# Polysketch attention and a multiplicative FFN on one core: queries, later keys and outputs transposed in 32x32 blocks by VectorE, from loads by head

## The chip, the cores and the metric

The kernel runs on one core of a Trainium2 chip. The metric is the device time of one execution in microseconds (us), lower is better. The engines are TensorE (PE; PEld are its weight loads), VectorE (DVE), ScalarE (ACT), GpSimd (POOL) and SyncE (SP), which issues the transfers. A profile is of one of the timed executions, and its span is 1.7 to 1.9 us shorter than that execution's time.

## The reference

```python
# q, k, v: (B=4, H=4, S=1088, D=32); S1, S2: (8, 32)
def phi(x):
    a = np.einsum('rd,bhsd->bhsr', S1, x)
    b = np.einsum('rd,bhsd->bhsr', S2, x)
    return np.einsum('bhsi,bhsj->bhsij', a, b).reshape(*x.shape[:-1], r * r)
q_p, k_p = (phi(q), phi(k))
kv = np.einsum('bhsf,bhsd->bhfd', k_p, v)
z = np.sum(k_p, axis=2)
num = np.einsum('bhsf,bhfd->bhsd', q_p, kv)
den = np.einsum('bhsf,bhf->bhs', q_p, z)[..., None] + 1e-06
x = (num / den).transpose(0, 2, 1, 3).reshape(B * S, H * D)      # 4352 tokens x 128
# w1, w2: (128, 1024); w3: (1024, 1024); w_out: (1024, 128), float64
out = ((x @ w1) * (x @ w2) @ w3) @ w_out
```

Nothing nonlinear stands between w3 and w_out, so the kernel multiplies the two once into one matrix w3o and saves the largest product. The weights come as float64 words; ScalarE and VectorE turn them into float32 in the kernel (raw, cv_c, cv_m, w3c in the profile).

## The kernel before

The tokens are worked off in nine groups: two halves of 512 tokens for each of four batches, and a last group of 256 with the 64 left-over tokens of each. A query goes through a long chain: transpose, projection, denominators, features, and the product with the keys' sums, which gives xT, the FFN's input. The FFN of a group is 8 pairs of products a and b, a VectorE product ab of each pair, and 8 products ps_o that add up the output, transposed. These are the transposes, each a copy, four products with the identity and a second copy:

```python
    def natural(t, half):                      # keys and queries: gather 512 tokens on ScalarE
        n = work.tile([128, 4, H, D], F32, tag="nat", name="nat")
        nc.scalar.copy(n, bview(t[:, 0, 4 * half], [[D, 4], [NJ * D, H], [1, D]]))
        return n.rearrange("p j h d -> p j (h d)")
    # ... in k_feat
        def tr():
            chunks = state.pop("chunks")
            ps = psum.tile([128, 512], F32, name="ps_kt", **banks)
            for j in range(nj):
                nc.tensor.transpose(ps[:, j * 128:(j + 1) * 128], chunks[j], ident)
            kT = work.tile([128, 512], F32, tag="kT", name="kT")
            nc.scalar.copy(kT[:, :nj * 128], ps[:, :nj * 128])
    # ... in q_steps
        def tr():
            ps = psum.tile([128, 512], F32, tag="t", name="ps_qt")
            for j, c in enumerate(s["src"]):
                nc.tensor.transpose(ps[:, j * 128:(j + 1) * 128], c, ident)
            s["qT"] = wtile("qT", bufs=2)
            nc.scalar.copy(s["qT"], ps[:, :n])
    # ... the FFN's output
    def ffn_o(g, c):
        _, n, _ = groups[g]
        if c == 0:
            o_ps[g] = psum.tile([DM, 512], F32, tag="out", name="ps_o")
        nc.tensor.matmul(o_ps[g][:, :n], w3o[:, c], ab_sb.pop((g, c))[:, :n], start=c == 0, stop=c == NC - 1)
        if c == NC - 1:
            o_ps[g, "sb"] = work.tile([DM, 512], F32, tag="ob", bufs=1, name="ob")
            nc.scalar.copy(o_ps[g, "sb"][:, :n], o_ps[g][:, :n])

    def ffn_out(g):
        _, n, dst = groups[g]
        ps = psum.tile([128, 4, DM], F32, tag="h", bufs=3, name="ps_ot")
        nj = n // 128
        for j in range(nj):
            nc.tensor.transpose(ps[:, j], o_ps[g, "sb"][:, j * 128:(j + 1) * 128], ident)
        oT = work.tile([128, 4, DM], F32, tag="oT", name="oT")
        nc.scalar.copy(oT[:, :nj], ps[:, :nj])
        dst(oT)
```

A first part, up to group 0's last pair, has a fixed order on every engine; after it a scheduler chooses the order on each engine. In the first part `gs` are the Gram products of batch 0's keys, `kv` the products of key features and values (both ps_kvz in the profile), `pause(n)` n dummy products that keep TensorE's clock up, and `f[c]` the product pairs of group 0:

```python
    run_all([sk_words, sketch_pairs, nat0, peak, sketch_T, tr0, nat1, tr1, pause(4), ab0, ab1, r_nat, r_tr, first, second,
             sketch_P_mm, r_ab, pause(3), gs0, kp0, gs1, kp1, q_nat, kv0, r_kp, kv1, kvr, q_tr, pause(5),
             # ... (fin1 .. phi of the first queries)
             w_out[0][1], n_dens2, f[4], n_phi, w_out[1][1], f[5], n_phT, f[6], n_nd, f[7]])
    run(merge(ffn_steps(1, 16), k_steps(1), w_out[2:]))     # from here on the scheduler orders
```

`w_out` is the list of steps that convert w_out (wo) and w3, multiply them and copy w3o.

## Time and profile before

| | before |
|---|---|
| time, median of 3 runs | 321.59 us (320.5 to 321.72) |
| span of the profile | 317.9 us |
| start: to where group 0's last product ab begins | 56.5 us |
| second stage: to where the last copy of w3o begins | 54.5 us |
| third stage: to where the last output's copy out of PSUM begins | 200.4 us |
| tail: to the end | 6.5 us |

The four stages are cut by the same events in every kernel here, so that their lengths can be set side by side. The first line of the page gives busy time, share of the span and number of instructions of each engine.

```profile
PE 296.4 (93%) x2143; PEld 176.8 (56%) x2143; DVE 188.0 (59%) x482; ACT 141.6 (45%) x277; POOL 7.1 (2%) x12
```

Two lines of the list of TensorE's waits (us in total, times, longest):

```profile
PE ps_ph L735 <- DVE ph L726: 1.6, 2, 1.2
PE ps_c L673 <- POOL q L649: 1.5, 2, 0.8
```

The second are two waits of 0.76 us in the third stage, from 167.5 and 226.9 us on, for a step of GpSimd in the query chain: nearly all of its idle time. The first lie in the start, 0.34 us at 31 us and 1.24 us at 49 us. The chain of waits in the start (start, us, engine, tile):

```profile
12.66 1.98 PE ps_kvz L508 x99
14.65 1.36 issue
16.01 1.67 PE ps_kvz L508 x61
```

The key products begin at 12.66 and end at 17.68 us, with 1.36 us in the middle in which TensorE waits for nothing that the profile shows.

### The profile page before, as it was taken

Reading aid. Unit: us, or ns where it says so; the run is one execution under the profiler, and the core shown is the slowest. Engines: PE = TensorE matmul, PEld = TensorE weight load, DVE = VectorE, ACT = ScalarE, POOL = GpSimd, SP = SyncE. Lnnn points to the kernel's source line nnn. Section 1 sums busy time; section 2 is a strip of 40 time slices with the busy share of each in tenths; the row PEclk is TensorE's granted clock in tenths of the full one; section 3 lists DMA queues with packets and bytes.
Section 4 is the critical chain, followed back from the end, with each engine's and each line's share of the span. In section 5 each row is a group of like instructions: output and inputs, shape, how many; then the busy total and the mean of one; then the engine's idle time right before and its main releaser. Section 6 shows DMA issues by size and latency. Waiting matters only on the chain.

```text
span 317.9 us, 5394 instructions
## 1 busy us (share of the span) xinstructions
PE 296.4 (93%) x2143; PEld 176.8 (56%) x2143; DVE 188.0 (59%) x482; ACT 141.6 (45%) x277; POOL 7.1 (2%) x12
## 2 busy tenths in 40 slices
PE   6898898589999999999999999999999999999992
PEld 4777433268777855655645456554545544444581
DVE  6769785899999463686537438443661662462120
ACT  4266674777976233632252471333324424423131
POOL 0000000000000000100001010000100100000000
PEclk9999999969999999999999999999999999999998
DMA  5539893166542000000000000000000000000000
GB/s 163 186 78 328 235 324 129 48 201 215 201 134 68 2 1 33 2 1 2 35 0 0 0 36 2 0 2 34 0 2 0 33 0 0 36 0 0 33 35 17
DMA packets 15065, 20.80 MB, mean 65 GB/s; under 512 B 4032, under 2 KB 11456, under 8 KB 15040
## 3 DMA queue, kind: packets, MB, share of 16 engines
q1 hardware_dynamic: 15040, 20.46, 20.3%
q8 instruction: 17, 0.28, 0.3%
q14 instruction: 8, 0.07, 0.1%
HBM read 18.22 MB, written 2.23 MB: 64 GB/s over the span
## 4 chain that ended last, share of the span: by engine, by line
PE 82%; DVE 9%; ACT 4%; issue 2%; POOL 1%; POOLq 0%; DVEq 0%; ACTq 0%
PE ps_o L810 19%; PE a_ps L797 18%; PE b_ps L801 15%; PE ps_kvz L508 5%; PE ps_w3o L403 5%; PE ps_wt L396 3%; PE ps_x L752 3%; PE ps_c L675 2%; PE ps_ab L452 2%; PE ps_c L673 2%; PE ps_ph L735 2%; PE idle_ps L190 2%; PE ps_ot L820 1%; ACT q L644 1%; ACT q L645 1%
## 5 line engine op out<-in xcount | busy, mean ns | idle before, releaser
L803 DVE TENSOR_TENSOR ab<-ffa,b_ps 128x512 f32<-128x512 f32 (+1 forms) x72 | 47.3, 657 | 68.2 <-PE b_ps L801 57.3
L799 ACT COPY ffa<-a_ps 128x512 f32<-128x512 f32 (+1 forms) x72 | 40.4, 560 | 75.9 <-PE a_ps L797 75.6
L797 PE MATMUL a_ps<-xT,w 128*128 128x512 f32 (+1 forms) x144 | 72.4, 585 | 1.0 <-ACT xT L755 0.7
L801 PE MATMUL b_ps<-xT,w 128*128 128x512 f32 (+1 forms) x144 | 70.1, 568 | 0.0
L810 PE MATMUL ps_o<-ab,w3o 128*128 128x512 f32 (+1 forms) x144 | 69.9, 582 | 0.0
L801 PEld LDWEIGHTS b_ps<-xT,w 128*128 128x128 f32 x144 | 27.1, 191 | 29.0 <-issue 25.0
L810 PEld LDWEIGHTS ps_o<-ab,w3o 128*128 128x128 f32 x144 | 24.9, 190 | 21.0 <-issue 19.8
L797 PEld LDWEIGHTS a_ps<-xT,w 128*128 128x128 f32 x144 | 24.4, 193 | 17.9 <-issue 11.1
L276 DVE TENSOR_REDUCE g_q<-qT 128x1 f32<-128x512 f32 (+1 forms) x9 | 5.9, 654 | 27.4 <-ACT qT L633 27.4
L403 PEld LDWEIGHTS ps_w3o<-wo,w3T 128*128 128x128 f32 x128 | 15.7, 192 | 3.4 <-issue 2.6
L737 ACT COPY pT<-ps_ph 128x512 f32<-128x512 f32 (+1 forms) x18 | 9.2, 565 | 18.5 <-PE ps_ph L735 18.5
L244 ACT ACTIVATE cv_c<-raw 128x512 f32<-128x512 f32 x22 | 15.0, 682 | 3.1 <-DVE w3c L257 2.6
L403 PE MATMUL ps_w3o<-wo,w3T 128*128 128x128 f32 x128 | 16.0, 275 | 0.0
L245 ACT ACTIVATE cv_m<-raw 128x512 int32<-128x512 uint32 x22 | 15.0, 681 | 0.9 <-DVE wo L260 0.4
L673 PE MATMUL ps_c<-Rf,q 128*128 128x64 f32 (+1 forms) x72 | 12.4, 263 | 2.6 <-POOL q L649 1.5
L190 PE MATMUL idle_ps<-zeros 128*128 128x256 bf16 x95 | 13.1, 295 | 1.7 <-DVE zeros L185 1.7
L675 PE MATMUL ps_c<-Rl,qT 128*128 128x96 f32 (+1 forms) x72 | 13.9, 284 | 0.0
L673 PEld LDWEIGHTS ps_c<-Rf,q 128*128 128x128 f32 (+1 forms) x72 | 10.4, 185 | 5.5 <-POOL q L649 2.4
L649 POOL TENSOR_TENSOR q<-qT,q 128x512 f32<-128x512 f32 (+1 forms) x6 | 6.4, 1074 | 267.4 <-ACT q L645 245.2
L508 PE MATMUL ps_kvz<-kk 128*32 128x64 f32 x256 | 8.6, 236 | 4.0 <-DVE kk L492 4.0
L462 DVE TENSOR_TENSOR kp<-ps_ab,b_sb 128x1024 f32<-128x1024 f32 x8 | 9.7, 1221 | 3.9 <-ACT b_sb L456 3.9
L190 PEld LDWEIGHTS <-zeros 128*128 128x128 bf16 x95 | 10.0, 108 | 3.4 <-DVE zeros L185 1.7
(162 smaller groups left out, 381.9 us busy)
## 6 DMA issues: line engine op xcount, KB each, us to landing
raw<-in_moe_w_dram SPq DMA_DIRECT2D x20, 512.0 KB, 4.8
k_sb<-in_k_dram SPq DMA_DIRECT2D x4, 512.0 KB, 4.0
v_sb<-in_v_dram SPq DMA_DIRECT2D x4, 512.0 KB, 4.1
q_sb<-in_q_dram SPq DMA_DIRECT2D x4, 512.0 KB, 5.8
out_dram<-oT SPq DMA_DIRECT2D x8, 256.0 KB, 2.0
raw<-in_moe_w_out_dram SPq DMA_DIRECT2D x2, 512.0 KB, 8.4
k_sb<-in_k_dram SPq DMA_DIRECT2D x4, 32.0 KB, 3.7
vr<-in_v_dram SPq DMA_DIRECT2D x4, 32.0 KB, 6.6
```

Source lines behind the costliest of these rows:

```text
L190: nc.tensor.matmul(idle_ps[:, :n], zeros[:, :128], zeros[:, :n], start=True, stop=True)
L244: nc.scalar.mul(x["c"], hi.bitcast(F32), 2.0 ** -112)
L245: nc.scalar.mul(x["m"].bitcast(I32), lo.bitcast(U32), 2.0 ** -29)
L403: nc.tensor.matmul(ps, w3T[ko][:, c], wo[:, c], start=(c == 0), stop=(c == NC - 1))
L508: nc.tensor.matmul(out[h * D:(h + 1) * D], lhs, rhs, start=start, stop=stop, skip_group_check=True)
L673: nc.tensor.matmul(C[rows, :2, j], s["q2"][:, cols], cols_of(Rf, b), start=True, stop=False, skip_group_check=True)
L675: nc.tensor.matmul(C[rows, :, j], s["qT"][:, cols], cols_of(Rl, b), start=False, stop=True, skip_group_check=True)
L797: nc.tensor.matmul(a_ps[:, :n], w1[:, cols], xT[key], start=True, stop=True)
L799: nc.scalar.copy(a_sb[:, :n], a_ps[:, :n])
L801: nc.tensor.matmul(b_ps[:, :n], w2[:, cols], xT[key], start=True, stop=True)
L803: nc.vector.tensor_mul(ab[:, :n], a_sb[:, :n], b_ps[:, :n])
L810: nc.tensor.matmul(o_ps[g][:, :n], w3o[:, c], ab_sb.pop((g, c))[:, :n], start=c == 0, stop=c == NC - 1)
```

## The change

VectorE transposes only inside 32x32 blocks (the prediction below cites the page that says so). A head has 32 columns, so if a load puts head h on the partitions 32h to 32h+31, and consecutive tokens beside each other in each partition, then one VectorE instruction over 128x512 gives what four products with the identity and two copies gave: (head, column) on the partitions, tokens in the free dimension. The tokens of a group come out in another order, which doesn't matter as long as the output's store puts them back. The outputs, which lie transposed in PSUM, go the same way: VectorE transposes straight out of PSUM, and four stores of 128 B runs put them in place. Only the last group's output stays with TensorE, stored by one transfer instead of four. Batch 0's keys stay with TensorE too. Later keys are loaded a second time for it, by head.

Two further parts: the start is reordered, so that the Gram products follow directly behind the key features (`first`, `second`), with the sketch's product later and two pauses gone; and five conversion steps move from behind the first part into it, so that all of wo and the words of w3's first piece are converted there. (With the two that stood there before they are the seven steps of `out_st`.)

```diff
+    def load_by_head(which, b):
+        n = {"q": NT, "k": 32}[which] * D
+        t = io.tile([128, n], F32, tag=which + "h", bufs={"q": 2, "k": 1}[which], name=which + "h")
+        if which == "q":
+            nc.sync.dma_start(t, bass.AP(tensor=q.tensor, offset=b * H * S * D, ap=[[n, 128], [1, n]]))
+        else:
+            for h in range(H):
+                nc.sync.dma_start(t[h * 32:(h + 1) * 32],
+                                  bass.AP(tensor=k.tensor, offset=(b * H + h) * S * D, ap=[[n, 32], [1, n]]))
+        by_head[which, b] = t
... (k_feat)
         def tr():
+            kT = state["kT"] = work.tile([128, 512], F32, tag="kT", name="kT")
+            if blocks:
+                nc.vector.transpose(bview(kT, [[1, 4], [128, nj], [4, 32]]), blocks())
+                return
... (queries)
+        def transpose(qT):
+            t = by_head["q", b]
+            nc.vector.transpose(qT, t[:, half * 512:(half + 1) * 512])
+            if half == 1:
+                nc.vector.transpose(qT_rest[:, b * SR:(b + 1) * SR], t[:, SM:])
+                if b + 2 < B:
+                    load_by_head("q", b + 2)
... (outputs)
-            nc.sync.dma_start(bass.AP(tensor=out.tensor, offset=(b * S + half * 4) * DM,
-                                      ap=[[NJ * DM, 128], [1, 4 * DM]]),
-                              oT.rearrange("p j d -> p (j d)"))
+            for i in range(4):
+                nc.sync.dma_start(bass.AP(tensor=out.tensor, offset=(b * S + half * 16) * DM + i * 32,
+                                          ap=[[NT * DM, 32], [DM, 16], [1, 32]]),
+                                  oT[i * 32:(i + 1) * 32].rearrange("p (T d) -> p T d", d=32))
...
-        if c == NC - 1:
-            o_ps[g, "sb"] = work.tile([DM, 512], F32, tag="ob", bufs=1, name="ob")
-            nc.scalar.copy(o_ps[g, "sb"][:, :n], o_ps[g][:, :n])
+        if c == NC - 1 and g < NG - 1:
+            oT = work.tile([128, 512], F32, tag="oT", name="oT")
+            nc.vector.transpose(oT, o_ps[g])
+            dst(oT)
+    def last_out():                            # the last group: TensorE, one store
+        ob = work.tile([DM, 256], F32, tag="ob", bufs=1, name="ob")
+        nc.scalar.copy(bview(ob, [[1, 4], [128, 2], [4, 32]]), o_ps[g][:, :n])
...
+    out_st, w_out = fs(w_out[:7]), w_out[7:]
-    run_all([sk_words, sketch_pairs, nat0, peak, sketch_T, tr0, nat1, tr1, pause(4), ab0, ab1, r_nat, r_tr, first, second,
-             sketch_P_mm, r_ab, pause(3), gs0, kp0, gs1, kp1, q_nat, kv0, r_kp, kv1, kvr, q_tr, pause(5),
+    run_all([sk_words, sketch_pairs, nat0, nat1, peak, sketch_T, tr0, tr1, ab0, ab1, r_nat, r_tr, first, second,
+             gs0, r_ab, kp0, gs1, kp1, gr, r_kp, sketch_P_mm, kv0, kv1, kvr, q_tr, pause(5),
...
-             pause(16), N_pair, ay1, q_rem, v0, n_nat, v1, ay2, n_tr, pause(30), split, dens, dens2, phi, j0, a0, j1, a1, phT, nd,
+             pause(16), N_pair, ay1, q_rem, v0, v1, ay2, n_tr, pause(30), split, dens, dens2, phi, j0, a0, j1, a1, phT, nd,
...
-             w_out[0][1], n_dens2, f[4], n_phi, w_out[1][1], f[5], n_phT, f[6], n_nd, f[7]])
+             out_st[0], n_dens2, f[4], out_st[1], n_phi, f[5], *out_st[2:4], f[6], n_phT, n_nd, *out_st[4:7], f[7]])
```

(The lines of `run_all` are broken at other places here than in the file; `last_out` is cut. Left out are small parts: the Gram products of the left-over keys become a step of their own, `gr`, and the copies that gather batch 0's keys share the buffers of w3's pieces.)

## The prediction

> **What bounds the kernel now.** I first read the busy digits and the granted clock by slice of the page (40 slices of 7.95 us), to see which engine is full in which stage.
>
> ```profile
> PE   6898898589999999999999999999999999999992
> ...
> DVE  6769785899999463686537438443661662462120
> ...
> PEclk9999999969999999999999999999999999999998
> ```
>
> The reader is to see four stages. Slices 0 to 6 (to about 57 us) are a start in which no engine is full: a chain of latencies. In slices 7 to 12 (57 to 101 us) VectorE stands at 8 and 9, and in slice 8 TensorE falls to 5 and its clock to 6. From slice 13 on TensorE is at 9 everywhere and VectorE at 3 to 8. The last slice is a tail. The page's chain that ended last agrees: PE 82%, DVE 9%, ACT 4%.
>
> For the second stage I asked for the busy time by stretch (per stretch: length, then busy us of PE, weight load, DVE, ACT, POOL, the clock, the DMA share, GB/s) and the list of waits (total us, times, longest).
>
> ```profile
> 60.00:70.00 10.00, 5.81 (x78) 4.15 (x78) 10.00 (x20) 6.49 (x12) 0.00 (x0) 0.66 0.56 166
> 70.00:80.00 10.00, 10.00 (x97) 8.04 (x96) 9.03 (x16) 8.15 (x16) 0.00 (x0) 1.00 0.66 211
> 80.00:101.00 21.00, 21.00 (x242) 15.72 (x242) 20.36 (x46) 16.83 (x33) 0.00 (x0) 1.00 0.45 148
> ```
>
> ```profile
> PE ps_kvz L508 <- DVE kk L492: 4.0, 1, 4.0
> ```
>
> VectorE is busy for all of 60 to 70 us, and TensorE idles 4.0 us of it in one piece, because the Gram products of batch 1 wait for kk, which stands in VectorE's queue behind the conversion of the output weights (wo). After that gap the clock is down: four transposes take 1.11 us in the chain at 66 us, against 0.44 later.
>
> For the long third stage I read the chain in order of time (start, us) and the groups by form (busy us, mean ns of one, idle before).
>
> ```profile
> 184.40 0.44 PE ps_ot L820 x4
> 184.83 0.44 PE ps_qt L631 x4
> ...
> 187.85 0.44 PE ps_kt L443 x4
> ```
>
> ```profile
> L820 PE MATMUL ps_ot<-ident,ob 128*128 128x128 f32 x34 | 5.2, 274 | 0.5 <-ACT ob L813 0.5
> L443 PE MATMUL ps_kt<-ident,nat 128*128 128x128 f32 x32 | 4.9, 277 | 1.2 <-ACT nat L108 1.2
> L631 PE MATMUL ps_qt<-ident,nat 128*128 128x128 f32 x32 | 4.9, 274 | 0.0
> ```
>
> The mean of 274 ns is the latency of one; they are pipelined, so what a set of four costs the engine is the chain's 0.44 us. They lie on the chain itself with nothing idle before them: whatever leaves TensorE here leaves the span.
>
> **What the Trainium skill says.** "VectorE: DVE Perf Modes", section "The three transpose paths": VectorE transposes only 32x32 blocks, 311 ns for 128x128 bf16 against TensorE's 390. No transpose of VectorE is in this trace. "Vector Engine (DVE) Microarchitecture Reference", section 3.8, has it sustain one element per cycle per lane. I therefore take the 0.69 us that this trace shows for other 128x512 f32 work on VectorE (L803: 686 ns), as an estimate. "TensorE: Matmul & The Clock Gate", Part 1: the clock halves after an idle window of about 3.4 us. The trace agrees: idle 4.0 us, granted 0.66 in that stretch, and 1.00 in every full one. "DMA: Bandwidth & Descriptors", Specifications: under 512 B a write is done as read-modify-write and misses line rate. The trace is only suggestive: 32 KB loads in 128 B runs took 3.7 to 6.6 us to land, 32 KB stores in 512 B runs 1.9 us, but the loads had other traffic beside them.
>
> **The change part by part.**
>
> (1) TensorE loses its transposes of queries (8 sets of four and 2 for the rest), of the keys of batches 1 to 3 (6 sets) and of outputs 0 to 7 (8 sets): 90 instructions at 0.11 us. In the third stage lie 6 of the query sets and the two, 4 key sets and 8 output sets: 18 x 0.44 + 0.22 = 8.1 us, all on the path. The other four sets lie in stages that TensorE doesn't bound.
>
> (2) ScalarE loses 14 natural-order copies (0.62), 8 qT copies (0.59) and the small one, 6 kT (0.58) and 8 each of ob and oT (0.585): 8.7 + 5.1 + 3.5 + 9.4 = 26.7 of its 141.6 us. By itself that is worth nothing in the third stage (ACT about 35% there). It shortens the head of each query chain: three times TensorE stood about 0.8 us before ps_c, waiting for q on POOL behind ACT's copies. I allow 0.5 us in all.
>
> (3) VectorE gains 22 transposes of 128x512 at 0.69 us and 4 small ones of 64 columns (about 0.22): 16.1 us, 188 to 204 us. In the third stage it has some 40% free. But its queue is in order: the transpose of an output waits there for the last ps_o product, and what stands behind it, the denominators of the queries, comes later. The bank of ps_o is single; the next group's first product must wait for the transpose where formerly it waited for an ACT copy of 0.59 us. Most times a pair of products (1.72 us) lies between. I set a loss of 1.5 us for such new waits.
>
> (4) Second stage: seven steps of the weight conversion, with both joins and adds of wo, move into the first part. At the pace of the chain (0.34 + 0.60 + 0.60) that takes 2 x 1.54 = 3.1 us of VectorE ahead of kk, and puts them into slots at 51 to 56 us where VectorE idled 2.16 and 2.23 us before two ab products. The two key transposes add 2 x 0.6. So kk should come some 3 us earlier, the gap of 4.0 us should become about 1, and the clock should stay up (it cost about 2 us: two sets of transposes at 1.11 for 0.44, and a product pair at 1.52 for 0.86). Against this, VectorE over 57 to 101 us is itself 96% full and wins only 3.1 - 1.2 = 1.9 us, unless it drops work done there early for batches 2 and 3. Between 1.9 and 5 us I choose 3.5.
>
> (5) Start: the Gram products follow the key features directly. Today kk is done at about 10.9 us and the Gram products begin at 12.6, behind pauses and the sketch product; keys' products end at 17.7. Taking away four pause products and letting the second natural copy run behind the first brings the ab products about 0.7 us forward. I expect the end of the key products at about 15.9 rather than 17.7 us (1.4 us of issue gap at 14.65 may stay). Against it, the second half's transpose and the rest of the queries now stand on VectorE in the chain at 25 us: 0.6 + 0.2 us. Net 1.0. At 49 us TensorE stood 1.24 us waiting for ph; the new order gives it product pair 6 first: another 1.0.
>
> (6) Tail: the last store is one transfer instead of four.
>
> ```profile
> 312.72 2.46 SPq L785 DMA_DIRECT2D out_dram<-oT  x4
> ```
>
> Each issue costs about 0.6 us, so the last left 1.8 us after the first: 1.8 us saved. The price is in the other outputs: four transfers a group, 2048 runs of 128 B instead of 128 of 2 KB. The queue was nearly empty after 101 us, and the last of these leaves some 8 us before the end.
>
> (7) Keys of batches 1 to 3 are loaded twice and queries in 4,352 B runs: 1.5 MB more, one third of it in the busy stretch of 24 to 48 us, where at some 300 GB/s it delays what follows by about 1.7 us. The list of waits shows no conversion waiting for its weights, so this is hidden.
>
> Sum: 8.1 + 0.5 - 1.5 + 3.5 + 1.0 + 1.0 + 1.8 = 14.4 us. 321.6 - 14.4 = 307.2; I say **307 us**.
>
> **The rivals.** (a) VectorE becomes a bound: if it needs two cycles an element for f32 transposes or for the strided key output, it gains some 28 us instead of 16, and the second stage gives back what it won; TensorE would then wait in the third stage at the four stretches where VectorE is at 6 to 8. The time would be about 313. For it: VectorE's 9s in slices 8 to 12. Against: the one element per cycle quoted above, and the 3s and 4s of most later slices. (b) A new wait takes the removed work's place: head-of-line waiting behind the output transposes delays the query chain and TensorE goes idle before ps_ph or ps_o; about 311. For it: today's chain lets a query chain pass at 104 to 124 us with barely any slack (VectorE's ph ends at 122.1 and TensorE takes it at 122.3). Against: the order after the first part is chosen again by the scheduler. (c) The small stores hold up the end: if 2048 runs took over 8 us, the last store would wait behind them; about 310. (d) The second stage gains fully, with the clock: 304 or less.
>
> **Range and chances.** Certain are the 8.1 us of part 1 and nearly so the 1.8 of the tail: 311.7 without anything else. The soft terms are the second stage (1.9 to 5), the start (0 to 3.5) and the new waits (0 to 5). All bad gives about 313, all good 301; I take 302 to 312.5. Two per cent is 315.2, which needs a slow VectorE transpose: faster 0.93, within 2% 0.06, slower 0.01.
>
> **What would show it.** Right, if the changed profile has TensorE's instructions 90 fewer and its digits still at 9 after slice 13, with that stage 7 to 9 us shorter; VectorE transposes of 128x512 near 0.69 us; the wait of ps_kvz for kk at 1 to 2 us and the clock digit of slice 8 back at 9; key products ending near 16 us; one last store. Wrong, if those transposes last 1 us or more, if TensorE shows new idle time before ps_o, ps_ph or ps_ab with VectorE as releaser, if the second stage is no shorter, or if the end waits for group 7's stores.

## More of the kernel before

The busy times by stretch, for exactly the third stage (length, then busy us and number for PE, PEld, DVE, ACT and POOL, the clock, DMA share, GB/s):

```profile
111.00:311.40 200.40, 198.71 (x1177) 107.42 (x1175) 98.44 (x248) 72.10 (x135) 6.44 (x6) 1.00 0.03 11
```

TensorE is idle for 1.69 of 200.40 us; VectorE is half free.

## The result, and the profile after

| | before | after |
|---|---|---|
| time, median of 4 runs each, taken in turn | 321.04 us (319.95 to 321.72) | **303.88 us** (303.19 to 304.54) |
| ratio after/before | | 0.947 (0.943 to 0.951) |
| span of the profile | 317.9 us | 301.4 us |
| start | 56.5 | 54.9 |
| second stage | 54.5 | 51.4 |
| third stage | 200.4 | 190.5 |
| tail | 6.5 | 4.6 |

A ratio here and below is the mean time of one kernel's fast runs over that of the other's of the same rounds, so it is not quite the ratio of the medians that stand beside it; the interval is the 95% one. The changed kernel is 17.2 us faster by the medians, 16.5 by the spans: 1.6 in the start, 3.1 in the second stage, 9.9 in the third, 1.9 in the tail. (The profiled runs were of 319.66 and 303.19 us.)

From the page of the changed kernel, the busy line, the digits of the same rows as shown of before, and the lines on transfers (the last is: output from tile, transfers, KB each, median us from issue to landing):

```profile
PE 285.5 (95%) x2046; PEld 168.1 (56%) x2046; DVE 202.8 (67%) x508; ACT 118.1 (39%) x232; POOL 7.6 (3%) x12
...
PE   7987799589999999999999999999999999999994
...
DVE  6989789989999975788559428645762573443131
...
PEclk9999999979999999999999999999999999999999
...
DMA packets 28584, 22.36 MB, mean 74 GB/s; under 512 B 19856, under 2 KB 25104, under 8 KB 28560
...
out_dram<-oT SPq DMA_DIRECT2D x32, 64.0 KB, 1.9
```

TensorE has 97 instructions fewer, the 90 transposes and 7 pauses. ScalarE has the 45 fewer that were expected; its busy time fell by 23.5 us, where the groups of removed copies sum to 26.9, because the page counts overlapping instructions once. VectorE gained 14.8 us; its digits are 3 to 8 in 21 of the 26 slices from the 15th on. Packets under 512 B went from 4,032 (the page of before) to 19,856, and the stores land as soon as before: 1.9 us for 64 KB, where the page of before gives 2.0 for its 256 KB ones.

The groups by form show VectorE's new instructions (line, engine, operation, out<-in, shapes, count, then busy us, mean ns of one, and idle time before them):

```profile
L460 DVE STREAM_TRANSPOSE kT<-kh 128x512 f32<-128x512 f32 x6 | 6.7, 1116 | 0.0
L833 DVE STREAM_TRANSPOSE oT<-ps_o 128x512 f32<-128x512 f32 x8 | 5.7, 716 | 2.4 <-PE ps_o L829 2.0
L783 DVE STREAM_TRANSPOSE qT<-qh 128x512 f32<-128x512 f32 x8 | 5.5, 702 | 1.3 <-PE ps_c L696 1.3
```

Queries take 0.702 us and outputs, out of PSUM, 0.716, as estimated (0.69). The keys' take 1.116.

The busy times by stretch, around the entry to the second stage and for exactly the third:

```profile
55.00:60.00 5.00, 1.80 (x7) 0.71 (x6) 5.00 (x11) 3.46 (x6) 0.00 (x0) 1.00 0.70 208
60.00:70.00 10.00, 8.79 (x66) 7.45 (x66) 9.21 (x16) 6.27 (x13) 0.00 (x0) 0.83 0.50 159
...
106.30:296.80 190.50, 190.38 (x1106) 100.55 (x1104) 107.13 (x257) 52.47 (x99) 6.86 (x6) 1.00 0.08 15
```

In the third stage TensorE's work fell from 198.71 to 190.38 us, so 8.3, and its idle time from 1.69 to 0.12 us, so 1.6: together the 9.9 us. In the second stage the hole is still there, moved forward: TensorE works 1.80 of 5 us where VectorE is busy without a break, and then the clock is down to 0.83. The list of TensorE's waits (us in total, times, longest) says for what:

```profile
PE ps_wt L412 <- ACT cv_c L260: 3.2, 1, 3.2
...
PE ps_ph L756 <- DVE ph L747: 1.5, 1, 1.5
PE ps_wt L412 <- DVE w3c L276: 1.2, 1, 1.2
...
PE ps_kvz L528 <- DVE kk L512: 0.3, 1, 0.3
```

The wait for kk went from 4.0 to 0.3 us, but the transposes of w3 (ps_wt) now wait 3.2 and 1.2 us for w3's conversion, which ends on VectorE. (The release by "ACT cv_c" is an inferred one: VectorE was busy for all of 55 to 60 us, ScalarE for 3.46 of it, and VectorE's last step for that piece of w3 ends at 59.30 us, just before the transposes begin at 59.45.)

The chain of waits in the start, and the end of the store in order of time:

```profile
10.93 0.99 PE ps_kvz L528 x41
...
14.77 1.32 PE ps_kvz L528 x72
```

```profile
298.34 0.62 SPq L804 DMA_DIRECT2D out_dram<-oT  x1
```

The Gram products begin at 10.93 us, and the key products end at 16.09 us instead of 17.68. One issue of 0.62 us stands where four took 2.46.

### The profile page after: what moved, and what is told of

It is laid out like the page before. It is cut to its first block, busy times and chain, and to the rows that moved or that the text cites. A ratio compares the mean times of both kernels' runs of the same rounds, so it can differ in the third digit from the quotient of the medians.

```text
span 301.4 us, 5229 instructions
## 1 busy us (share of the span) xinstructions
PE 285.5 (95%) x2046; PEld 168.1 (56%) x2046; DVE 202.8 (67%) x508; ACT 118.1 (39%) x232; POOL 7.6 (3%) x12
## 2 busy tenths in 40 slices
DMA packets 28584, 22.36 MB, mean 74 GB/s; under 512 B 19856, under 2 KB 25104, under 8 KB 28560
## 4 chain that ended last, share of the span: by engine, by line
PE 82%; DVE 10%; ACT 3%; issue 2%; DMA 1%; SPq 1%; DVEq 0%
PE a_ps L816 19%; PE ps_o L829 19%; PE b_ps L820 18%; PE ps_w3o L419 5%; PE ps_kvz L528 5%; PE ps_x L773 3%; PE ps_wt L412 3%; PE ps_c L696 2%; PE ps_c L694 2%; PE ps_ph L756 2%; PE ps_ab L472 2%; DMA k_sb<-in_k_dram 1%; DVE g_k L292 1%; DVE g_q L292 1%; ACT ffa L818 1%
## 5 line engine op out<-in xcount | busy, mean ns | idle before, releaser
L419 PEld LDWEIGHTS ps_w3o<-wo,w3T 128*128 128x128 f32 x128 | 16.8, 206 | 1.6 <-issue 0.9
L419 PE MATMUL ps_w3o<-wo,w3T 128*128 128x128 f32 x128 | 17.5, 291 | 0.0
L261 ACT ACTIVATE cv_m<-raw 128x512 int32<-128x512 uint32 x22 | 14.8, 678 | 1.4 <-DVE w3c L276 1.3
L412 PE MATMUL ps_wt<-ident,w3c 128*128 128x128 f32 x64 | 10.6, 288 | 4.4 <-ACT cv_c L260 3.2
L696 PE MATMUL ps_c<-Rl,qT 128*128 128x96 f32 x64 | 13.2, 288 | 0.0
L412 PEld LDWEIGHTS ps_wt<-ident,w3c 128*128 128x128 f32 x64 | 7.8, 149 | 9.4 <-ACT cv_c L260 4.2
L776 ACT COPY xT<-ps_x 128x512 f32<-128x512 f32 (+1 forms) x9 | 5.1, 561 | 19.1 <-PE ps_x L773 19.1
L756 PEld LDWEIGHTS ps_ph<-ident,ph 128*128 128x128 f32 x68 | 7.9, 140 | 6.3 <-issue 4.8
```

The lines of the kernel that those rows point to most:

```text
L412: nc.tensor.transpose(ps[:, c], w3c[i][:, c * 128:(c + 1) * 128], ident)
L419: nc.tensor.matmul(ps, w3T[ko][:, c], wo[:, c], start=(c == 0), stop=(c == NC - 1))
L696: nc.tensor.matmul(C[rows, :, j], s["qT"][:, cols], cols_of(Rl, b), start=False, stop=True, skip_group_check=True)
```

## The experiments

The theory: the third stage is TensorE's, so each transpose taken from it counts in full, and VectorE has room for it; the second stage is VectorE's, so moving wo's conversion closes the hole only in part; start and tail add what was expected. The rivals: VectorE's new work is itself paid for somewhere; the keys' slow transposes cost time; the gain of the second stage is the clock's, or is the scheduler's; the start's gain is lost on the way. The experiments start from the changed kernel, gave correct results, and were timed in alternation with the kernel before. Ratios are to that kernel; the changed kernel has 0.947.

| run | median us (range, runs) | ratio (95%) | start | second | third | tail |
|---|---|---|---|---|---|---|
| changed kernel | 303.88 (303.19 to 304.54, 4) | 0.947 (0.943 to 0.951) | 54.9 | 51.4 | 190.5 | 4.6 |
| e1_keys_contig | 303.99 (303.05 to 304.83, 5) | 0.947 (0.944 to 0.950) | 56.8 | 51.1 | 190.5 | 4.6 |
| e2_k1_pe | 304.25 (303.28 to 306.68, 6) | 0.948 (0.945 to 0.952) | 55.2 | 49.9 | 191.8 | 4.7 |
| e3_out_pe | 307.94 (307.02 to 308.99, 6) | 0.959 (0.956 to 0.962) | 55.2 | 52.4 | 194.6 | 4.6 |
| e4_dve_double | 303.75 (303.35 to 305.39, 5) | 0.947 (0.944 to 0.950) | 56.9 | 51.0 | 191.1 | 4.6 |
| e5_wo_back | 309.43 (309.29 to 310.90, 5) | 0.967 (0.965 to 0.970) | 56.7 | 57.2 | 190.4 | 4.6 |
| e6_start_old | 305.29 (304.49 to 306.89, 6) | 0.953 (0.950 to 0.955) | 58.1 | 51.8 | 190.6 | 4.6 |
| e7_tail4 | 306.85 (306.77 to 307.41, 4) | 0.958 (0.956 to 0.960) | 56.7 | 51.0 | 190.6 | 6.8 |
| e8_q_out_pe | 314.83 (314.29 to 316.68, 6) | 0.984 (0.981 to 0.987) | 56.7 | 52.1 | 200.2 | 5.9 |
| e9_pause | 301.85 (301.65 to 302.11, 6) | 0.942 (0.940 to 0.944) | 55.0 | 50.0 | 190.5 | 4.6 |
| e10_ntr_late | 303.29 (302.99 to 303.67, 5) | 0.947 (0.944 to 0.949) | 55.3 | 51.3 | 190.6 | 4.6 |
| e11_combined | 301.49 (301.27 to 301.85, 5) | 0.941 (0.939 to 0.944) | 54.7 | 49.8 | 190.5 | 4.6 |
| e12_w3_first | 301.66 (301.37 to 303.42, 6) | 0.941 (0.936 to 0.945) | 54.5 | 51.7 | 188.8 | 4.6 |

The stages are of the one profiled run of each, which for e1, e3, e4, e5, e6 and e8 was among its slowest. The start is either about 55 or about 57 us in kernels whose first part is the same, and that has to be read first. In e7 below, which differs from the changed kernel only in the last store, TensorE waits the same 1.51 us for ph at 29 us as in the changed kernel. Then come these 4 us, in the changed kernel and in e7:

```profile
32.00:36.00 4.00, 3.31 (x8) 1.06 (x8) 2.37 (x6) 2.50 (x5) 0.00 (x0) 1.00 1.09 331
```

```profile
32.00:36.00 4.00, 3.32 (x6) 0.93 (x6) 2.14 (x5) 1.91 (x4) 0.00 (x0) 0.50 1.08 338
```

The clock is 1.00 in one and 0.50 in the other, after the same waits. It costs some 1.8 us, from run to run. What decides it is not shown: e9 below has the same wait of 1.51 us, and all six of its runs have a mean clock of 0.998 or more. (The runs were made on different chips, each in alternation with the kernel before.) So a start of 56.7 instead of 54.9 us says nothing of an edit that doesn't touch the start, and the second and third stages are compared beside it.

### e3_out_pe: the outputs back to TensorE

The eight outputs go through a ScalarE copy, four TensorE transposes and another copy again, and one store of 2 KB runs.

```diff
-            oT = work.tile([128, 512], F32, tag="oT", name="oT")
-            nc.vector.transpose(oT, o_ps[g])
-            dst(oT)
+            ob = o_ps[g, "sb"] = work.tile([DM, 512], F32, tag="ob", bufs=1, name="ob")
+            nc.scalar.copy(bview(ob, [[1, 4], [128, 4], [4, 32]]), o_ps[g])
+    def ffn_out(g):
+        ...
+        for u in range(4):
+            nc.tensor.transpose(ps[:, u], ob[:, u * 128:(u + 1) * 128], ident)
+        nc.scalar.copy(oT, ps.rearrange("p u d -> p (u d)"))
```

> Only the outputs of groups 0 to 7 go back to TensorE, with two ScalarE copies and stores in 2 KB runs. Theory (from 100 us on the span is TensorE's work, a set of four transposes is 0.44 us of it): 8 x 0.44 = 3.5 us slower than the changed kernel, ratio to before about 0.958. Rival (the gain of the third stage came from shorter query chains and a freer ScalarE, not from TensorE's work): 0 to 1.5 us slower, 0.947 to 0.952.

Measured: 307.94 us, 4.1 more than the changed kernel. The third stage by stretch:

```profile
107.60:302.20 194.60, 193.71 (x1138) 103.38 (x1136) 102.01 (x249) 64.79 (x115) 6.86 (x6) 1.00 0.04 14
```

TensorE's work grew from 190.38 to 193.71, so 3.3 us (8 x 0.44 were expected to be 3.5), and its idle time from 0.12 to 0.89. The third stage is 4.1 us longer, which is the whole difference in time. So the transposes do lie in full on the path, and the ScalarE copy makes TensorE wait (0.9 us before ps_o, for ob) where VectorE's transpose does not. (That copy is slower here than in the kernel before, 1,083 ns against 586, because it writes every fourth element. The second stage also read 1.0 us longer in this profile; the clock of its 60 to 70 us was 0.66, against 0.83 in the changed kernel's.)

### e8_q_out_pe: queries and outputs back to TensorE

Beside the outputs, all queries and the rest go back to the loads, copies, transposes and stores of the kernel before; the keys, the conversions and the order of the start's key products stay as changed.

```diff
-            nc.vector.transpose(qT, t[:, half * 512:(half + 1) * 512])
+            nat = natural(q_sb[b], half)
+            ...
+            for j, c in enumerate(transpose()):
+                nc.tensor.transpose(ps[:, j * 128:(j + 1) * 128], c, ident)
+            nc.scalar.copy(s["qT"], ps[:, :n])
```

> Queries and outputs both go back to TensorE and ScalarE, in natural order with four last stores; keys, start and conversions stay changed. Against the run with outputs alone put back, the third stage should gain 6 x 0.44 + 0.22 = 2.9 us from TensorE's work and up to 1.7 us if the waits of ps_c for the query chain return (theory: they were caused by the longer chain through ScalarE); the tail 1.8 us. Total against the changed kernel: 3.5 + 2.9 + 1.7 + 1.8 = 9.9 us, ratio 0.978. Rival (those waits come from POOL and not from the chain, and stay away): 8.2 us, 0.972.

Measured: 314.83 us, 6.9 more than e3 and 11.0 more than the changed kernel, where 9.9 or 8.2 had been expected. The third stage takes 5.6 us more than in e3, start and tail 1.5 and 1.3 (its tail has the old four stores). The profiled run is its slowest, 316.68 us. In the third stage TensorE's work rose by 4.3 us to 198.00, and its idle time to 2.20. Six query sets and the two transposes of the rest account for 2.9 of the 4.3; the remaining 1.4 is work that the scheduler took from the second stage or that I can't assign. A wait that the changed kernel no longer has is back, with three stretches up to 0.8 us:

```profile
PE ps_c L696 <- POOL q L672: 2.1, 3, 0.8
```

So the queries' transposes were worth more than their products: the copies on ScalarE ahead of GpSimd's step kept TensorE waiting, 1.5 us in the kernel before and 2.1 here.

The difference that is left between e8 and the kernel before is 5.8 us by the medians. The profiles, of e8's slowest run and of one of the kernel before that was under its median, hold 3.0 of it: second and third stage together take 2.6 us less than before, nearly all of it in the second, and the tail 0.6. The four key sets of the third stage alone should have given 1.8 us there; with the shifted work they don't show, and I did not isolate them.

### e4_dve_double: VectorE's transposes done twice

The queries' transposes of batches 1 to 3 and the outputs' transposes are written twice: 14 more instructions, 9.9 us more of VectorE, at the places where the new ones stand.

```diff
+            if b >= 1:
+                nc.vector.transpose(qT, t[:, half * 512:(half + 1) * 512])
...
             nc.vector.transpose(oT, o_ps[g])
+            nc.vector.transpose(oT, o_ps[g])
```

> Each VectorE transpose of an output and of a query of batches 1 to 3 is done twice (14 more of 0.7 us, 9.9 us of VectorE). Theory (they lie beside TensorE's work): within 1 us of the changed kernel, ratio to before 0.946 to 0.951. Rival (VectorE is on the path in the third stage): 5 to 10 us slower, 0.962 to 0.978.

Measured: 303.75 us against 303.88. The doubles took 717 and 702 ns each, as the first ones; second and third stage together took 242.1 us instead of 241.9. The one new wait for them is this:

```profile
PE ps_o L831 <- DVE oT L836: 1.0, 1, 1.0
```

So VectorE has room for twice this work in the third stage, and the waits that I had allowed 1.5 us for cost nothing that can be seen. The rivals by which VectorE becomes a bound, or head-of-line waits behind the output transposes take their share, fall.

### e1_keys_contig: the keys' transpose written in one piece

Batches 1 to 3 lay a head's keys out in a different order in the load, so that the transposes write kT in one piece and not every fourth element.

```diff
-                nc.vector.transpose(bview(kT, [[1, 4], [128, nj], [4, 32]]), blocks())
+                nc.vector.transpose(kT, blocks())
```

(The load gets a third dimension, and `blocks()` the view that goes with it.)

> The keys by head are loaded in 1 KB runs in another order, so that VectorE's key transposes write their output in one piece instead of with a stride of four elements. Theory (the stride made them slow, 1.12 us against 0.70 of the query transposes): they fall to about 0.70 us. If VectorE bounds the stage from 55 to 100 us, two of them there are worth 0.8 us of the span; if TensorE or the loads bound it, 0. Ratio to the kernel before 0.944 to 0.947. Rival (the f32 input in pieces is what costs): they stay at 1.1 us.

```profile
L461 DVE STREAM_TRANSPOSE kT<-kh 128x512 f32<-128x512 f32 x6 | 4.2, 704 | 0.0
```

The transposes went from 1,116 to 704 ns, so the strided output is what they had cost, 0.41 us each. The time did not move (303.99 us). Second and third stage together are 0.3 us shorter, less than the runs differ. A cost on VectorE that is cut by 2.5 us in all, 0.8 of it in the second stage, is not seen at this resolution.

### e2_k1_pe: batch 1's keys back to TensorE

```diff
-        load_by_head("k", 1)
-            feats.append(k_feat(chunk, 4, None, "t" if b else "h", blocks if b else None))
+            feats.append(k_feat(chunk, 4, None, "t" if b else "h", blocks if b > 1 else None))
```

> Only the keys of batch 1 go back to TensorE and ScalarE (no second load of them). VectorE loses 2 x 1.12 us in the stage of 55 to 100 us, TensorE gains 2 x 0.44, ScalarE 2.4, the loads lose 0.5 MB. If VectorE bounds this stage: 1 to 2 us faster than the changed kernel (ratio to before about 0.942). If TensorE does: 0.9 us slower (0.950).

Measured: 304.25 us. In the stretch 60 to 70 us TensorE was busy for 9.53 of 10 us and the clock stayed at 1.00. The second stage took 1.5 us less, and the third 1.3 more: in this order TensorE waits 2.5 us for ph in all instead of 1.5. Of the 1.3 us, 0.9 are idle time (0.12 to 1.05) and 0.4 work (190.38 to 190.75). Neither of the two expectations came true. Moving batch 1's keys to VectorE is neither a gain nor a loss that these runs, whose times spread over 3.4 us, can show.

### e5_wo_back: wo's conversion behind the first part again

```diff
-    out_st, w_out = fs(w_out[:7]), w_out[7:]
+    out_st, w_out = fs(w_out[:2]), w_out[2:]
```

(And the five further steps leave the list of the first part.)

> Five of the seven weight conversion steps moved ahead (both joins and adds of wo, the words of the first w3 tile) go back behind the first part. Theory (VectorE is full from 55 to 70 us, so 3.1 us of it moved into idle slots is worth that much): 2 to 3.5 us slower than the changed kernel, ratio to before 0.953 to 0.958. Rival (the gap of TensorE only changed its name, and the second stage got shorter for another reason: ScalarE's 26 us or the key path): less than 1 us slower, up to 0.950.

Measured: 309.43 us, 5.5 more, where 2 to 3.5 had been expected. The stretch 60 to 70 us and the wait are those of the kernel before, and worse, since VectorE now has the key transposes as well:

```profile
60.00:70.00 10.00, 4.91 (x67) 4.24 (x68) 10.00 (x20) 5.43 (x10) 0.00 (x0) 0.63 0.52 159
```

```profile
PE ps_kvz L528 <- DVE kk L512: 6.6, 2, 6.2
```

So step (4) of the prediction is right in its cause: moving the conversion is worth 5.5 us in the changed kernel. Without it, the change would have lost 2.7 us in the second stage instead of gaining 3.1.

### e9_pause: dummy products in the hole

28 dummy products behind `f[7]`, which change no data. In the trace they run from 54.5 to 57.6 us; the two products a and b that stood there in the changed kernel run behind them, up to the first transposes of w3 at 59.46 us (59.45 in the changed kernel). So TensorE's hole at 56 to 59 us is filled, and nothing waits longer.

```diff
-              ... *out_st[4:7], f[7]])
+              ... *out_st[4:7], f[7], pause(28)])
```

> 28 dummy products (bf16, 128x256, 0.11 us each) follow the first part on TensorE, in the gap of 4.4 us before the first transposes of w3, to keep its clock up; nothing else changes. Theory (that gap costs itself and, through the clock, some 1.8 us more: 16 products of w3o took 3.0 us instead of 1.8, four transposes 1.07 instead of 0.44): 1.5 to 2 us faster than the changed kernel, ratio to before about 0.941. Rival (VectorE is full there, so a faster TensorE only waits more): within 0.5 us, 0.946.

Measured: 301.85 us, 2.0 less than the changed kernel, and the six runs lie within 0.5 us. The clock of the stretch 60 to 70 us is 1.00. After the hole the chain of waits goes on so (start, us, engine, tile), in the changed kernel and then in e9:

```profile
61.28 1.07 PE ps_wt L412 x4
62.36 3.00 PE ps_w3o L419 x16
```

```profile
61.47 0.63 PE ps_wt L412 x4
62.10 1.84 PE ps_w3o L419 x16
```

Four transposes took 0.63 instead of 1.07 us, and sixteen products 1.84 instead of 3.00: 1.6 us, the second stage's difference being 1.4. So of what was left in the hole, this much is the clock's and can be had by dummy products alone. The Trainium skill, "TensorE: Matmul & The Clock Gate", section "HAM oscillation — how this bites in real kernels", warns of idle gaps over some 3.4 us; here a gap of 3.2 us and one of 1.2 us close behind it were enough.

### e12_w3_first and e11_combined: w3's conversion into the first part too

e11 joins e1, e9 and e10 (below). e12 is e11 with six more conversion steps, those of w3's first chunks, in the first part behind `f[7]`.

```diff
-    out_st, w_out = fs(w_out[:7]), w_out[7:]
+    out_st, w_out = fs(w_out[:13]), w_out[13:]
-              ... *out_st[4:7], f[7], pause(28)])
+              ... *out_st[4:7], f[7], *out_st[7:], pause(12)])
```

> The two edits above and the key transposes in one piece together. Theory (they act at different places): 2.5 to 4 us faster than the changed kernel, 300 to 301.5 us, ratio 0.934 to 0.939. Rival (one bound behind all of them, VectorE to 70 us): as good as the better of the two alone, 0.941 or more.

> As the combined version, but six more conversion steps (words of w3 tiles 1 and 2, joins and adds of tiles 0 and 1) close the first part, ahead of batch 1's key maximum on VectorE, and the pause is 12 products. Theory (TensorE's work from 55 us on starts with the transposes of w3, which wait for VectorE's first two tiles): the first of them starts near 57 instead of 59.2 us, the second near 59 instead of 61.2, and the second stage is 1.5 to 2.5 us shorter than the combined version's 49.8; 299 to 300 us, ratio to before 0.934 to 0.937. Rival (VectorE's total from 55 to 100 us sets the stage, whatever the order): within 0.5 us of the combined version, 0.941.

Measured: 301.49 and 301.66 us. TensorE's instructions in order of time show that e12 did what it was to do (e11 first, then e12):

```profile
59.19 0.66 PE L413 MATMUL ps_wt<-ident,w3c 128*128 128x128 f32 x4
```

```profile
57.04 0.66 PE L413 MATMUL ps_wt<-ident,w3c 128*128 128x128 f32 x4 [1.58 <-DVE w3c L277]
```

The first transposes of w3 begin 2.15 us earlier, yet second and third stage together take 240.5 us in e12 and 240.3 in e11. (Some output products come earlier in e12 and move the border between the two stages, so only the sum compares.) What begins earlier waits elsewhere: TensorE's idle time in the two stages is 1.6 us in e11 and 3.1 in e12 (1.6 before the first transposes, then 0.9 for w3o and 0.6 for an output's transpose), while 2.7 us of dummy products became 0.95. The busy times over 57 to 101 us, e11 first:

```profile
57.00:101.00 44.00, 42.47 (x460) 31.93 (x459) 42.75 (x92) 32.07 (x61) 0.00 (x0) 1.00 0.52 158
```

```profile
57.00:101.00 44.00, 43.10 (x451) 31.83 (x452) 41.41 (x88) 31.14 (x60) 0.00 (x0) 1.00 0.51 157
```

VectorE is nearly full in both (42.75 and 41.41 of 44 us), but so is TensorE (42.47, 0.40 of it dummy products, and 43.10). The result is the one that was expected if VectorE's sum sets the stage, whatever the order; but TensorE's own work would give it as well, and no run parts the two.

e11 and e12 are the fastest kernels here, 2.4 and 2.2 us under the changed one by the medians (0.941 against 0.947). e9 alone gives nearly all of that.

### e6_start_old: the start's order as before

```diff
-    run_all([sk_words, sketch_pairs, nat0, nat1, peak, sketch_T, tr0, tr1, ab0, ab1, r_nat, r_tr, first, second,
-             gs0, r_ab, kp0, gs1, kp1, gr, r_kp, sketch_P_mm, kv0, kv1, kvr, q_tr, pause(5),
+    run_all([sk_words, sketch_pairs, nat0, peak, sketch_T, tr0, nat1, tr1, pause(4), ab0, ab1, r_nat, r_tr, first, second,
+             sketch_P_mm, r_ab, pause(3), gs0, kp0, gs1, kp1, kv0, r_kp, kv1, gr, kvr, q_tr, pause(5),
```

> The order of the first 18 us is put back as it was (second natural copy later, pauses, sketch product ahead, Gram products behind them). Theory: the key products end 1.6 us later and all of it reaches the end, ratio to before 0.952. Rival (what follows waits for something else, such as the sketch chain or the loads): the products end later, the end does not, 0.947.

Measured: 305.29 us, 1.4 more; the means give 1.9 (0.953 against 0.947, of 321). The profile is of its slowest run (306.89). There the chain of waits has the pause in the middle of the key products again:

```profile
15.72 1.92 issue
17.65 1.67 PE ps_kvz L528 x61
```

The key products end at 19.32 us, 3.2 later than in the changed kernel, and the start as a whole is 3.2 us longer. So the start's reordering reaches the end, with 1.4 to 1.9 us. In the kernel before the same pause is 1.36 us long, most of the 1.59 us by which the key products end earlier after the change. Why TensorE stands still there for 1.4 to 1.9 us in the old order and not in the new one, the profile doesn't say; it stays open.

### e10_ntr_late: the second half's query transpose behind the features

In the changed kernel VectorE transposes the second half's queries (0.70 us) and the rest (0.23) ahead of the first half's features, and TensorE's wait for ph grew from 0.34 us in the kernel before to 1.51.

```diff
-              pause(16), N_pair, ay1, q_rem, v0, v1, ay2, n_tr, pause(30), split, dens, dens2, phi, j0, a0, j1, a1,
+              pause(16), N_pair, ay1, q_rem, v0, v1, ay2, pause(30), split, dens, dens2, phi, n_tr, j0, a0, j1, a1,
```

> The transposes of batch 0's second half and rest go behind phi on VectorE, so that they no longer stand in the chain at 24 us. Theory (they cost 0.75 us there and opened an idle gap of 1.5 us on TensorE, in which the clock falls in some of the runs): ps_ph comes 0.75 us earlier, the runs with a clock of 0.98 and 1.8 us more get rarer; 0.7 to 1.7 us faster, ratio 0.941 to 0.945. Rival (the second half's chain waits for them then): no gain, 0.947.

```profile
PE ps_ph L756 <- DVE ph L747: 0.8, 1, 0.8
```

The wait was halved and the time did not follow: 303.29 us, ratio 0.947 as before. The start's end came no earlier (55.3 us). The second half's chain waits for its transpose instead, as the rival said: TensorE's list has a new wait of 0.5 us for a query step of ScalarE. That the low clock at 32 us would get rarer was not tested: none of these five runs shows it, but none of e9's does either, with the long wait.

### e7_tail4: the last store in four transfers

```diff
-        nc.sync.dma_start(bass.AP(tensor=out.tensor, offset=(NT - 2) * DM,
-                                  ap=[[NT * DM, 32], [S * DM, B], [1, 2 * DM]]), oT.rearrange("p u d -> p (u d)"))
+        for i in range(4):
+            nc.sync.dma_start(bass.AP(tensor=out.tensor, offset=(NT - 2 + 8 * i * NT) * DM,
+                                      ap=[[NT * DM, 8], [S * DM, B], [1, 2 * DM]]),
+                              oT[i * 32:(i + 1) * 32].rearrange("p u d -> p (u d)"))
```

> The last store goes out as four transfers of 32 partitions instead of one of 128. Theory (each issue costs about 0.6 us on the queue and the end waits for the last): 1.8 us slower than the changed kernel, ratio 0.952. Rival (the end is set by the landing of all bytes, not by the issues): below 0.5 us, 0.947 to 0.948.

```profile
299.83 2.93 SPq L805 DMA_DIRECT2D out_dram<-oT  x4
```

The four issues took 2.93 us instead of the one's 0.62, and the tail 6.8 instead of 4.6: 2.2 us. The median rose by 3.0 us (306.85). The clock of 0.50 at 32 to 36 us, which cost its profile 1.8 us, is the likely other part: all four of its runs have a mean clock of 0.977 to 0.985, where the changed kernel's have 0.987 to 0.993. That is a correlation and not shown by an experiment.

## Why the prediction was right

The time was predicted at 307 us (302 to 312.5) and is 303.9. The gain of 14.4 us became 17.2 in time and 16.5 in span. By steps, in us of span:

| step | predicted | measured | from |
|---|---|---|---|
| (1) TensorE's transposes in the third stage | 8.1 | 8.3 | busy 198.71 to 190.38 |
| (2), (3) waits there: queries +0.5, VectorE −1.5 | −1.0 | +1.6 | idle 1.69 to 0.12 |
| (4) second stage | 3.5 | 3.1 | 54.5 to 51.4 |
| (5) start | 2.0 | 1.6 | 56.5 to 54.9 |
| (6) tail | 1.8 | 1.9 | 6.5 to 4.6 |
| (7) more and smaller transfers | 0 | 0 | stores land in 1.9 us |

- **(1) was right** in kind and size. e3 puts 8 of the 18 sets back and pays 3.3 us of work for 3.5 expected.
- **(2) and (3) are the term that was mis-sized, by 2.6 us**, and that is the whole surplus of the gain in span (2.1 us) once the 0.5 us by which the other steps together fell short is set against it. It also made the third stage 9.9 us shorter, where 7 to 9 had been named as the sign of being right. "I set a loss of 1.5 us for such new waits": the changed kernel's list has none (e4, e5 and e12 have one each, of 0.6 to 1.0 us). e4 doubles the work in question and second and third stage grow by 0.2 us. "I allow 0.5 us in all" for the queries' shorter chain: the waits for GpSimd's step were 1.5 us before (two of 0.76, not three as the prediction read), 2.1 in e8, and are gone. I had put both terms as if the idle time of the third stage could only go up a little or down a little; it could go down by all of the 1.69 us that the view of before showed.
- **(4) had the right cause and size, and the wrong picture after it.** kk came early (0.3 us of wait; I had expected 1 to 2), and e5 shows the move to be worth 5.5 us. But "the gap of 4.0 us should become about 1, and the clock should stay up" failed: the gap came back as 3.2 and 1.2 us before ps_wt and the clock fell to 0.83 (the page's digit of slice 8 is 7, not 9). I had looked at what stood ahead of kk, and not at what would be next to wait for the same queue. So that the sum came near 3.5 us is in part luck: the hole and its clock stayed, and the middle of a wide range (1.9 to 5) was met. The stated counterweight, that VectorE's sum hardly falls, fits e12 but is not shown by it; e9 shows 2.0 us more to be had by dummy products. (Five steps moved and not seven, and the two key transposes took 1.1 us each and not 0.6; the 3.1 us of joins and adds was counted rightly.)
- **(5) was right in sum, in part by luck.** The key products end at 16.09 us for 15.9 predicted, 1.59 earlier; but 1.36 of that is as much as the issue gap that I thought might stay and whose cause is open. The loss by the queries' transposes on VectorE was there (the wait for ph, 0.34 to 1.51 us, so 1.2 for 0.8), and the other wait for ph, 1.24 us at 49 us, is gone as predicted: 1.6 − 1.2 + 1.2 = 1.6. e10 shows that moving the transposes gains nothing. That some runs would have a low clock behind the longer wait, for 1.8 us, was not foreseen; that the wait is the cause isn't shown.
- **(6) and (7) were right**: 2.2 us in e7, and no store that holds the end up.
- **The rivals.** (a) A VectorE that becomes the bound: the strided key transposes did take 1.116 us, over the 1 us that I had named as the sign of it, yet they were six only, and e1 shows that nothing hangs on them; fallen by e4. (b) Head-of-line waits: fallen by e4. (c) Small stores: fallen. (d) The second stage gains fully with the clock, 304 us or less: the time came true (303.9), but not by this way. The second stage gained 3.1 us with the clock at 0.83, and it was the third stage's waits that made up the rest. What (d) describes is nearer to e9, 301.85 us.

## What to carry to other kernels

When one engine is full for a long stage, count a removed instruction at what it occupies in the chain (0.44 us for four pipelined transposes, not 4 x 274 ns), and look at that stage's idle time as a further gain if the waits in it hang on the work that is removed. Where an in-order queue of another engine feeds the full one, look past the wait that you remove to the next consumer of the same queue: here the hole moved to it, and what could still be had was the clock's share, by a few dummy products. Before you compare a stage between two profiles, check that the clock before it was the same.

## What the Trainium skill lacked or had wrong

- "VectorE: DVE Perf Modes", section "The three transpose paths", has one size and type for VectorE (128x128 bf16, 311 ns). The runs show 702 ns for 128x512 f32 out of SBUF and 716 ns out of PSUM, and that the blocks alone are enough where the head has 32 columns. "Useful for some layouts" could name this one.
- "SBUF — State Buffer", section "Door 1: The DMA port swizzle", says that accesses which leave a 16-byte line pay a penalty, but gives no size. The runs agree with it and give one: writing every fourth f32, VectorE's transpose took 1,116 ns instead of 704 (e1), and ScalarE's 128x512 copy out of PSUM 1,083 ns (e3) instead of the 586 ns that the kernel before took in one piece.
- "DMA: Bandwidth & Descriptors", Specifications, warns of writes under 512 B. On a nearly empty queue, 64 KB stores in 128 B runs landed in 1.9 us, no later than 256 KB stores in 2 KB runs (2.0 us), which carry four times as much each; the page doesn't say when the penalty is hidden.
- "TensorE: Matmul & The Clock Gate", Part 1, has the clock fall after an idle window of about 3.4 us. Here it fell to 0.50 in some runs, at a cost of some 1.8 us: in e7 about 1.6 us after the end of a gap of 1.51 us, ahead of which TensorE had been busy for 7.48 of 8 us. In other runs with the same gap it did not fall. That the gap is the cause isn't shown. The page's free-running window would let it vary from run to run, but does not say how short a gap can be enough.
- No page that I found gives, for this chip, how the cost of issuing a transfer from SyncE depends on its shape. Here the median issue took 0.33 us for 256 KB in 2 KB runs and 0.49 us for 64 KB in 128 B runs; the last store took 0.62 us as one transfer and 2.93 us as four (e7), on the path at the end of the kernel.
